# A four-layer attention and Fourier-mixing kernel: another rule for the steps at which QKV groups are issued

## The chip, the cores and the metric

The kernel runs on one core of one Trainium2 chip. The core has five engines with a queue each, worked off in order: TensorE (PE, matmuls and transposes into the eight PSUM banks), VectorE (DVE), ScalarE (ACT), GpSimd (POOL) and SyncE (SP), which issues nearly all DMAs here. The metric is the device time of one execution in microseconds; the time before is the median of 3 runs.

## What is computed

Four layers on x of 2048 x 640 (float32), attention, Fourier, attention, Fourier, each added to its input after a layer norm:

```python
def _A_ref(x, wqkv, wo):          # H = 32 heads of 20, W = 8, dil = 2
    qkv = (x @ wqkv).reshape(B, S, 3, H, Dh)...
    idx = pos[:, None] - (jnp.arange(W) * dil)[None, :]
    logits = jnp.einsum("bhsd,bhswd->bhsw", q, kg) * scale   # kg = k at idx
    logits = jnp.where(mask, logits, -1e9)
    o = jnp.einsum("bhsw,bhswd->bhsd", softmax(logits), vg)
    return o @ wo

def _B_ref(x, re_s, im_s, re_h, im_h):
    a, b = x @ re_h.T, x @ im_h.T
    return re_s @ a - im_s @ b

x = x + _A_ref(_layernorm(x), wqkv, wo)
x = x + _B_ref(_layernorm(x), ...)
x = x + _A_ref(_layernorm(x), wqkv, wo)
x = x + _B_ref(_layernorm(x), ...)
```

Every matmul is made of three passes on operands that are split into a high part and a residue.

## The kernel before

**Tiling.** The sequence is cut into NC = 4 chunks of NJ = 4 tiles of 128 tokens. The QKV weights are cut into NQ = 4 quarters (8 heads each). A *QKV group* is one chunk c, quarter q and tile j: `qkv_mm` (L346) runs 15 matmuls (L356) of 128x480 into PSUM bank m0 or m1 by the parity of the group's number, `qkv_evac` (L359) copies the bank to a staging tile `stg` (two buffers) on ScalarE (L363), and after each second tile `qkv_store` (L365) writes K, V (`kvb`) and Q (`qb`) to DRAM. There are 64 groups in an attention layer.

**Attention units.** A unit u (0 to 31) is one chunk and four heads. `q_load` (L384) and `w_load` (L401) read Q and the eight shifted K or V rows back from DRAM; `q_copy` (L398) puts Q into PSUM bank pq on ScalarE; `qk_mul` (L422) multiplies on VectorE (L425) and adds halves on POOL (L427); `qk_red` (L433), the softmax pieces `soft` (L443 to L459) and `soft_exp` (L441, on ScalarE) follow; `av_mul` (L463) multiplies by V on VectorE and `av_tree` (L478 to L480) sums on POOL.

**Other TensorE work of a layer.** A tile of x is loaded (`x_load`, tag `xa`, two buffers), normalized on ScalarE (`x_norm`, L185), transposed (`tp`: L321 on TensorE, high part L325 on ScalarE, subtraction of it in PSUM L329 on TensorE, residue L344 on ScalarE). The first chunk's tiles are ready ahead of the steps, the twelve of chunks 1 to 3 are transposed at steps `tx[(c, j)]`. The output product `wo_mm` (L503) runs in two halves per tile, two and three steps after the steps in `OUTP`, and `wo_add` (L153) adds its result on VectorE.

**The plan.** Both attention layers are one long list of steps, -7 to 66. `at(step, phase, fn, ...)` enters a piece; at the end, steps are walked in order, and in each step the phases in the order of `PHASES` (L815). This fixes the order on all five engines, SyncE's queue included. Unit u takes steps 2u and 2u + 1 for `qk_mul`, the next ones for softmax and V. `q_copy` of unit u stands in step 2u - 1, in phase `qc`, after the phases `evac`, `hi`, `exp`, `evacA`, `actL`, `evacO`, `actl`, all of which are ScalarE's. A group of an odd step is evacuated in phase `evac` of the next step; a group of an even step in `evacA` of its own step, or, if the group before it has the same step, in `evacO` of the next.

**The steps of groups.** `order` lists the 64 groups; `gs` gets a step for each. The first 16 come from `LEAD0` (layer 0) or `LEAD2` (layer 2). The rest is filled in by the loop over `st`: two groups in an even step, one in an odd step or in a step listed in `THIN`, as soon as the tile's transposes are in an earlier step. Transposes may be placed in even steps, one tile per step, once all groups on that tile's buffer (the same j of the chunk before) are in earlier steps.

```python
            cap = 0 if st < 6 else 2 if st % 2 == 0 and st not in THIN[ly] else 1
            for _ in range(max(0, cap - gs[:16].count(st))):
                if len(gs) < NGRP and len(gs) <= 16 + st and tx.get(order[len(gs)][::2], st) < st:
                    gs.append(st)
```

The loads of unit u stand in steps 2u - 2 (`q_load` in phase `dma`, `w_load` of K in `dmaw`) and 2u + 1 (`w_load` of V); a store of a group from step 6 on stands in phase `dmas`, which comes after `dma` and `dmaw` of the same step.

Of the kernel before, what the change touches and what calls it, by code (L numbers as in the profile page):

```python
# [27 lines left out]
NC = 4  # L28
NJ = 4
NQ = 4  # L30
# [8 lines left out]

THIN = ((20, 24, 26, 28, 32, 36, 40, 44), (12, 16, 20, 24, 28, 32, 36, 44, 48))  # L40
OUTP = (((20, 24, 28, 32), (36, 40, 44, 46)), ((20, 24, 28, 32), (36, 40, 44, 46)))
LNS = ((40, 52), (40, 52))


LEAD2 = (-7, -6, -5, -4, -2, 0, 0, 1, 1, 2, 3, 4, 4, 6, 6, 7)
ZTHIRDS = (
# [27 lines left out]
def tile_layers(ctx: ExitStack, tc: tile.TileContext, x, wqkv, wo, cs, wre, wim, out):  # L74
# [158 lines left out]
    NGRP = NC * NQ * NJ  # L233
    ENGINES = {e.engine for e in (nc.tensor, nc.vector, nc.scalar, nc.gpsimd, nc.sync)}

    def layer_a(li, stats, handoff, prev):
        xin, xout = xs[li], xs[li + 1]
        first = li == 0
        ly = li // 2
# [431 lines left out]
        for k in range(KD):  # L671
# [6 lines left out]
        order = [(0, q, j) for q in range(NQ) for j in range(NJ)]  # L678
        order += [
            (c, 2 * qh + i, 2 * jh + j)  # L680
            for c in range(1, NC)
            for qh in range(2)
            for jh in range(2)
            for i in range(2)
            for j in range(2)
        ]
        gs = list(LEAD0 if first else LEAD2)
        tx = {(0, j): -8 for j in range(NJ)}
        st = 4
        while len(gs) < NGRP:  # L690
            if st % 2 == 0 and len(tx) < NC * NJ:
                c, j = divmod(len(tx), NJ)
                used = [i for i, x in enumerate(order) if x[0] == c - 1 and x[2] == j]
                if used[-1] < len(gs) and gs[used[-1]] < st:
                    tx[(c, j)] = st
            cap = 0 if st < 6 else 2 if st % 2 == 0 and st not in THIN[ly] else 1
            for _ in range(max(0, cap - gs[:16].count(st))):
                if len(gs) < NGRP and len(gs) <= 16 + st and tx.get(order[len(gs)][::2], st) < st:
                    gs.append(st)
            st += 1  # L700
        for g, cqj in enumerate(order):
# [27 lines left out]
        for c in range(1, NC):  # L729
            for j in range(NJ):  # L730
                b = tx[(c, j)]
                at(b - 4, "dma", x_load, c, j)
                if first:
                    at(b - 3, "actl", x_stats, c, j)
                    at(b - 2, "fin", x_fin, c, j)
                at(b - 1, "actl", x_norm, c, j)
                tp(b, "x", c, j, 0, 4, "xt", 0, f"s{j}")
                tp(b, "x", c, j, 4, 5, "t1", 256)
# [602 lines left out]
```

## Time and profile before

| | |
|---|---|
| median of 3 runs | 1803.96 us (1803.42 to 1805.32) |
| the profiled execution, its own time | 1805.26 us |
| its span, first to last instruction | 1803.4 us |
| granted TensorE clock, mean | 0.994 |
| layer 0's attention, T(0) to T(63) | 34.0 to 371.9 us |
| layer 2's attention, T(0) to T(63) | 936.8 to 1263.4 us |
| TensorE busy in the Fourier part, 395 to 900 us | 497.4 of 505 |
| DMA, mean rate | 236 GB/s |

T(s) is the start of step s's L425. A row of busy time by stretch reads: the stretch and its length, then for each engine the busy time and the count of instructions, then the granted clock, the mean busy share of the 16 DMA engines and GB/s. A row of the chain of waits reads: start, duration, and what ran or was waited for. A row of the timeline reads: start, duration, engine, line, operation, out<-in, shape, count, and in brackets the idle time ahead of it with what ended it. Matmuls are pipelined, so a group's time on TensorE is the distance between starts (3.25 us for 15), not the sum of their durations.

### The profile page before, as it was taken

The page shows a single profiled execution, that of the slowest core. Times are in us where ns is not written, and L with a number is a line of the kernel's source. Part 1 is how long each engine was busy: PE and PEld are TensorE (multiplying, and loading weights), DVE is VectorE, ACT ScalarE, POOL GpSimd, SP SyncE. Part 2 cuts the span into 40 slices and gives each one's busy share as a digit, 9 for nine tenths or more (in the row PEclk, how much of TensorE's full clock was granted, in tenths as well). Part 3 has the DMA queues.
Part 4 walks back from the last instruction along what each step waited for, and adds up shares of the span by engine and source line. Part 5 has one row for each costly group of instructions (what it writes and reads, how often), then busy time and mean ns, then how long its engine had stood idle before and what let it go on. Part 6 is the DMA issues. An engine that isn't in the chain of part 4 may idle for free.

```text
span 1803.4 us, 26465 instructions
## 1 busy us (share of the span) xinstructions
PE 1743.7 (97%) x8798; PEld 1505.7 (83%) x8798; DVE 1382.3 (77%) x2129; ACT 816.8 (45%) x1702; POOL 633.5 (35%) x591
## 2 busy tenths in 40 slices
PE   9999997989999999999999999999899999999999
PEld 6878896877888888888888889878787888888888
DVE  5999899887767767767739987889777676676673
ACT  5654544444445445445523434444534443443441
POOL 3899898950000000000018987899300000000000
PEclk9999998999999999999999999999999999999999
DMA  6896667847777787777647766687687766866861
GB/s 238 280 312 209 211 202 245 273 166 280 261 253 254 247 269 253 240 269 256 224 134 232 258 191 194 204 307 260 205 300 264 251 222 228 266 231 221 261 208 52
DMA packets 271849, 425.15 MB, mean 236 GB/s; under 512 B 22592, under 2 KB 150592, under 8 KB 271456
## 3 DMA queue, kind: packets, MB, share of 16 engines
q1 hardware_dynamic: 268512, 421.49, 70.5%
q10 hardware_dynamic: 3200, 1.97, 0.4%
q8 instruction: 70, 1.15, 0.3%
q14 instruction: 67, 0.55, 0.1%
HBM read 338.23 MB, written 85.14 MB: 235 GB/s over the span
## 4 chain that ended last, share of the span: by engine, by line
PE 64%; DVE 13%; DMA 9%; POOL 7%; issue 3%; ACT 3%; SPq 0%; DVEq 0%; ACTq 0%; POOLq 0%
PE m L356 15%; PE aux L1018 12%; PE t L1107 10%; PE m L1107 10%; PE pq L1107 5%; PE xt L1107 5%; PE aux L503 4%; DMA win<-cs_in 3%; DVE pr L425 2%; POOL pr L478 2%; DVE pr L463 2%; DMA xc<-stg 2%; POOL pr L427 2%; POOL r L876 1%; POOL pr L479 1%
## 5 line engine op out<-in xcount | busy, mean ns | idle before, releaser
L356 PE MATMUL m<-r,s 128*128 128x480 f32 x1920 | 438.3, 383 | 7.5 <-ACT stg L363 2.9
L356 PEld LDWEIGHTS m<-r,s 128*128 128x128 f32 x1920 | 355.9, 188 | 63.4 <-ACT stg L363 4.6
L1100 ACT CAST r<-win 128x512 fp32r<-128x512 f32 x248 | 151.6, 620 | 170.4 <-DVE win L1136 79.9
L168 POOL TENSOR_TENSOR stats<-stats,mhalf 128x1 f32<-128x1 f32 (+1 forms) x40 | 28.8, 719 | 564.5 <-ACT stats L164 564.5
L1018 PE MATMUL aux<-r2a,zo 128*128 128x320 f32 x768 | 226.4, 309 | 0.0
L478 POOL TENSOR_TENSOR pr<-pr 128x640 f32<-128x640 f32 x126 | 205.6, 1632 | 40.1 <-DVE pr L463 39.2
L1018 PE MATMUL aux<-pr,zo 128*128 128x320 f32 x704 | 208.2, 308 | 0.0
L425 DVE TENSOR_TENSOR pr<-pq,win 128x1280 f32<-128x1280 f32 x128 | 189.8, 1483 | 23.4 <-ACT pq L398 23.3
L1101 DVE TENSOR_TENSOR r<-win,r 128x512 fp32r<-128x512 f32 x248 | 167.3, 687 | 45.6 <-ACT r L1100 43.9
L463 DVE TENSOR_TENSOR pr<-pq,win 128x1280 f32<-128x1280 f32 x128 | 190.8, 1491 | 4.3
L427 POOL TENSOR_TENSOR pr<-pr 128x640 f32<-128x640 f32 x128 | 183.5, 1434 | 19.1 <-DVE pr L425 16.1
L1107 PE MATMUL m<-r,r 128*128 128x512 f32 x606 | 156.5, 392 | 1.0 <-DVE r L1101 0.9
L1018 PEld LDWEIGHTS aux<-r2a,zo 128*128 128x128 f32 x768 | 144.1, 188 | 2.0
L940 PE MATMUL m<-s,r 128*128 128x512 f32 x384 | 120.0, 400 | 16.6 <-DMA s<-c0b 5.3
L1107 PEld LDWEIGHTS m<-r,r 128*128 128x128 f32 x606 | 113.5, 188 | 26.9 <-DVE r L1101 1.2
L1018 PEld LDWEIGHTS aux<-pr,zo 128*128 128x128 f32 x704 | 132.2, 188 | 2.1
L1107 PE MATMUL t<-r,r 128*128 128x512 f32 x483 | 130.7, 393 | 2.1 <-issue 2.1
L940 PE MATMUL t<-s,r 128*128 128x512 f32 x384 | 118.1, 395 | 2.3 <-DVE ot L1000 1.5
L479 POOL TENSOR_TENSOR pr<-pr 128x320 f32<-128x320 f32 x126 | 113.7, 903 | 9.9
L363 ACT COPY stg<-m 128x480 f32<-128x480 f32 x128 | 71.1, 556 | 100.7 <-PE m L356 89.9
L433 DVE TENSOR_REDUCE lg<-pr 128x64 f32<-128x640 f32 x128 | 103.9, 812 | 13.8 <-POOL pr L427 13.6
L1107 PEld LDWEIGHTS t<-r,r 128*128 128x128 f32 x483 | 90.5, 188 | 23.6 <-issue 1.5
(274 smaller groups left out, 3231.2 us busy)
## 6 DMA issues: line engine op xcount, KB each, us to landing
win<-cs_in SPq DMA_DIRECT2D x354, 256.0 KB, 4.1
r<-xc SPq DMA_DIRECT2D x240, 256.0 KB, 4.2
win<-kvb SPq DMA_DIRECT2D x96, 440.0 KB, 4.7
xa<-cs_in SPq DMA_DIRECT2D x122, 256.0 KB, 3.9
win<-kvb SPq DMA_DIRECT2D x64, 360.0 KB, 5.1
xc<-stg SPq DMA_DIRECT2D x40, 512.0 KB, 4.6
kvb<-stg SPq DMA_DIRECT2D x60, 320.0 KB, 3.2
xr<-xs SPq DMA_DIRECT2D x40, 320.0 KB, 3.9
```

Source lines behind the costliest of these rows:

```text
L356: nc.tensor.matmul(mt[g][:, : 3 * F], st[:, a, k], wq[q][:, b, k], start=n == 0, stop=n == 14)
L425: nc.vector.tensor_tensor(pr, q, wview(u, jp, 0, [[1, FE]]), op=ALU.mult)
L427: nc.gpsimd.tensor_tensor(pv[:, :, 0:10], pv[:, :, 0:10], pv[:, :, 10:20], op=ALU.add)
L433: nc.vector.tensor_reduce(lgs[u][:, 2 * jp : 2 * jp + 2].rearrange("p j w h -> p (j w h)"), prq.pop((u, jp))[:, :, 0:10], axis=AX.X, op=AL ...
L463: nc.vector.tensor_tensor(pr.rearrange("p j w (h d) -> p j w h d", d=DH), lgs[u][:, 2 * jp : 2 * jp + 2].unsqueeze(4).to_broadcast([P, 2, ...
L478: g.tensor_tensor(pr[:, :, 0:4], pr[:, :, 0:4], pr[:, :, 4:8], op=ALU.add)
L479: g.tensor_tensor(pr[:, :, 0:2], pr[:, :, 0:2], pr[:, :, 2:4], op=ALU.add)
L940: self.last = nc.tensor.matmul(self.z[t][k], self.xn[c][:, a, j, k * P : (k + 1) * P], self.ct[s][:, b], start=s == 0 and i == 0, stop=s = ...
L1018: self.last = nc.tensor.matmul(self.ym[e][:, :320], zt[(k, a, ri)][:, j2 * P : (j2 + 1) * P], w[:, e * 320 : (e + 1) * 320], start=(k, a, ...
L1100: nc.scalar.copy(hi, raw)
L1101: nc.vector.tensor_tensor(lo, raw, hi.bitcast(F32), op=ALU.subtract)
L1107: nc.tensor.matmul(bank, w(a, kb), hl[b], start=start and (a, b) == (0, 0), stop=stop and (a, b) == (1, 0),)
```

## The change

It replaces `THIN` by a running sum of TensorE's work. `work` is all that stands in steps 6 to `QKV_END` = 46 (3.25 for a group, 0.83 for a tile's transposes, 0.8 and twice 2.2 for an output tile); `rate` is that by the number of steps; a group is entered into a step as long as the sum stays under the straight line `rate * (st - 5)` plus `AHEAD` = 2.4, at most two in any step, odd or even. `LEAD2` is shifted in three places. In layer 2 a tile's transposes may stand in step 5, 7, 8, 9, 10 and any later step. The order of groups in chunk 1 follows `QJ1`; in chunks 2 and 3 the pair of tiles is the outer loop and the quarter the inner. A tile's load is entered no earlier than the step in which the tile two before it in the chunk is transposed. `PHASES` and all functions that issue instructions are the same.

```diff
-THIN = ((20, 24, 26, 28, 32, 36, 40, 44), (12, 16, 20, 24, 28, 32, 36, 44, 48))
+QJ1 = ((0, 0), (1, 0), (0, 1), (2, 0), (1, 1), (3, 0), (2, 1), (3, 1))
+QKV_END = 46
+AHEAD = 2.4
...
-LEAD2 = (-7, -6, -5, -4, -2, 0, 0, 1, 1, 2, 3, 4, 4, 6, 6, 7)
+LEAD2 = (-7, -6, -5, -4, -2, -1, 0, 0, 1, 2, 3, 4, 4, 5, 6, 7)
...
         order = [(0, q, j) for q in range(NQ) for j in range(NJ)]
-        order += [
-            (c, 2 * qh + i, 2 * jh + j)
-            for c in range(1, NC)
-            for qh in range(2)
-            for jh in range(2)
-            for i in range(2)
-            for j in range(2)
-        ]
+        order += [(1, q, 2 * jh + j) for q, jh in QJ1 for j in range(2)]
+        order += [(c, q, 2 * jh + j) for c in range(2, NC) for jh in range(2) for q in range(NQ) for j in range(2)]
         gs = list(LEAD0 if first else LEAD2)
         tx = {(0, j): -8 for j in range(NJ)}
-        st = 4
-        while len(gs) < NGRP:
-            if st % 2 == 0 and len(tx) < NC * NJ:
+        other = {}
+        for c in range(2):
+            for a in OUTP[ly][c]:
+                for t, w in ((a, 0.8), (a + 2, 2.2), (a + 3, 2.2)):
+                    other[t] = other.get(t, 0) + w
+        work = sum(w for t, w in other.items() if 6 <= t <= QKV_END)
+        work += 3.25 * sum(g >= 6 for g in gs + [NGRP] * (NGRP - len(gs))) + 0.83 * (NC - 1) * NJ
+        rate = work / (QKV_END - 5)
+        done = 0
+        for st in range(4, 60):
+            if (st % 2 == 0 if first or st > 10 else st > 4 and st != 6) and len(tx) < NC * NJ:
                 c, j = divmod(len(tx), NJ)
                 used = [i for i, x in enumerate(order) if x[0] == c - 1 and x[2] == j]
                 if used[-1] < len(gs) and gs[used[-1]] < st:
                     tx[(c, j)] = st
-            cap = 0 if st < 6 else 2 if st % 2 == 0 and st not in THIN[ly] else 1
-            for _ in range(max(0, cap - gs[:16].count(st))):
-                if len(gs) < NGRP and len(gs) <= 16 + st and tx.get(order[len(gs)][::2], st) < st:
-                    gs.append(st)
-            st += 1
+                    done += 0.83
+            n = gs[:16].count(st)
+            if st >= 6:
+                done += other.get(st, 0) + 3.25 * n
+            while st >= 6 and n < 2 and len(gs) < NGRP and tx.get(order[len(gs)][::2], st) < st:
+                if done + 3.25 > rate * (st - 5) + AHEAD:
+                    break
+                gs.append(st)
+                done += 3.25
+                n += 1
+        assert len(gs) == NGRP
...
-                at(b - 4, "dma", x_load, c, j)
+                at(max(b - 4, tx.get((c, j - 2), 0)), "dma", x_load, c, j)
```

## The prediction

> **What bounds the kernel now.** I read the page first, then the busy time by stretch, then the chain of waits in both attention layers, then the order of single instructions where the chain leaves TensorE. "T(s)" below is the start of the first multiplication (L425, `qk_mul`) of step s; a step belongs to one half of one attention unit.
>
> ```profile
> span 1803.4 us, 26465 instructions
> PE 1743.7 (97%) x8798; PEld 1505.7 (83%) x8798; DVE 1382.3 (77%) x2129; ACT 816.8 (45%) x1702; POOL 633.5 (35%) x591
> PE 64%; DVE 13%; DMA 9%; POOL 7%; issue 3%; ACT 3%; SPq 0%; DVEq 0%; ACTq 0%; POOLq 0%
> ```
>
> TensorE holds most of the chain, but not all of it, so stretches have to be looked at by themselves. The next view gives, for each stretch, its length, then busy time of PE, PE's loads, DVE, ACT and POOL, the granted clock and DMA.
>
> ```profile
> 65.02:147.08 82.06, 76.97 (x371) 64.84 (x370) 78.45 (x103) 46.42 (x112) 75.91 (x71) 1.00 0.89 291
> 147.08:228.99 81.91, 81.87 (x440) 73.37 (x439) 73.51 (x108) 42.84 (x117) 73.03 (x70) 1.00 0.65 203
> 147.08:175.07 27.99, 27.99 (x157) 25.58 (x155) 27.27 (x41) 10.90 (x31) 26.21 (x25) 1.00 0.65 203
> 970.76:979.98 9.22, 9.22 (x50) 8.00 (x48) 8.96 (x13) 4.23 (x10) 8.81 (x9) 1.00 0.72 207
> 961.64:1035.17 73.53, 71.09 (x344) 61.50 (x343) 70.90 (x95) 29.44 (x69) 68.77 (x64) 0.98 0.78 253
> 1035.17:1169.31 134.14, 134.14 (x714) 120.57 (x713) 113.20 (x165) 56.72 (x144) 110.77 (x102) 1.00 0.61 195
> 993.17:996.58 3.41, 3.27 (x9) 2.75 (x10) 2.89 (x6) 1.22 (x5) 3.25 (x4) 0.50 0.85 330
> ```
>
> Rows 1 and 2 are steps 6 to 21 and 22 to 37 of layer 0: first VectorE is full (78.45 of 82.06) and TensorE has gaps, then TensorE is full and VectorE has gaps (73.51 of 81.91). Rows 5 and 6 are steps 6 to 21 and 22 to 45 of layer 2, with a much larger contrast (113.20 of 134.14). A pair of steps takes 9.2 us where VectorE sets it (row 4), 9.33 with output additions (row 3: three pairs). So there is something to even out. The chain shows where it turns:
>
> ```profile
> 126.74 2.10 POOL pr L478
> 145.27 3.25 PE m L356 x15
> 222.07 3.28 PE m L356 x15
> 228.99 1.49 DVE pr L425
> ```
>
> In layer 0 it is on VectorE and POOL until step 21 and on TensorE from 145 to 225 us. In layer 2:
>
> ```profile
> 909.90 3.11 PE m L356 x13
> 933.84 13.01 PE m L356 x60
> 983.94 8.17 DMA qb<-stg
> 992.21 0.56 ACT stg L363
> 994.21 20.72 PE m L356 x90
> 1014.93 0.44 PE xt L321 x4
> 1019.00 6.58 PE m L356 x30
> 1158.74 2.19 PE aux L503 x15
> 1161.49 3.26 PE m L356 x15
> 1168.86 0.43 ACT pq L398
> 1169.31 1.49 DVE pr L425
> ```
>
> From 994 to 1164.7 us it is TensorE without a break. A QKV group (15 matmuls, L356) is 3.25 us, half an output product 2.19. What ends it is the evacuation of the one group of step 44, then ScalarE's queue, then `q_copy` (L398) of step 45, then T(46) = 1169.31.
>
> **The change part by part.** The instructions are the same in kind and number; only steps move. I worked the step lists out from the rule itself. Groups finished by the end of a step, before and after:
>
>     step            5   9  12  13  16  21  28  30  36  44  45  47
>     layer 0 before 16  21  24  25  30  36  43  46  53  61  62  64
>     layer 0 after  16  21  25  27  31  38  45  46  53  62  64  64
>     layer 2 before 13  18  21  22  26  33  41  44  51  61  62  64
>     layer 2 after  14  19  24  26  30  37  44  46  53  62  64  64
>
> *Layer 0* is unchanged through step 10. The gaps that can be filled stand in TensorE's own list:
>
> ```profile
> 86.11 2.40 PE L356 MATMUL m<-r,s 128*128 128x480 f32 x10
> 89.86 4.58 PE L356 MATMUL m<-r,s 128*128 128x480 f32 x20 [1.36 <-ACT s L344]
> 96.65 3.54 PE L356 MATMUL m<-r,s 128*128 128x480 f32 x15 [2.20 <-ACT stg L363]
> 100.91 13.36 PE L356 MATMUL m<-r,s 128*128 128x480 f32 x60 [0.72 <-ACT stg L363]
> ```
>
> The first gap waits for a residue that the change doesn't move, and the 2.20 gap (bank m1 until step 12's evacuation) stays too: the second group that step 11 now has ends by about 94.2, in the place of the one that ran there. What goes are the 0.72 and the later pauses up to 145 us (0.5), and the order in steps 12 to 15 leaves no new ones: at 3.25 us a group and 0.83 us a transposed tile I get 37 groups at 145.7, with one tile more transposed; the old kernel had 36 at 144.2 and would have the same work done at 148.5. TensorE is 2.5 us ahead. Against it, step 14 gets two groups; the second is evacuated in step 15 ahead of `q_copy` (L398), at 117.0 rather than 110.7, and T(16) goes from 117.05 to about 120.7. VectorE is then 3.3 behind at step 22 and does steps 22 to 37 at 9.33 a pair plus the same 0.1 of slack: 147.08 + 3.3 + 8 x 9.45 = 226.0; by TensorE T(38) = 228.99 - 2.5 = 226.5. So layer 0 gains 2.5. Bounds: 5.5 gained if T(16) doesn't move (the least that VectorE needs is 147.08 + 75.6 = 222.7, and a little for jitter); 1 lost if both sides lag in turn.
>
> *Layer 2* has another start. Transposes of chunk 1 come in steps 5, 7, 8, 9 and not 6, 8, 10, 12, and step 6 issues groups 14 and 16 (032 and 100, chunk, weight quarter, tile), with 15 in step 7. Both of step 6 use bank m0. The ScalarE rows of the same place before:
>
> ```profile
> 961.18 0.43 ACT L398 COPY pq<-qs 128x320 f32<-128x320 f32 x1
> 965.50 0.31 ACT L441 ACTIVATE lg<-lg 128x128 f32<-128x128 f32 x1 [2.72 <-DVE lg L452]
> 965.72 0.54 ACT L363 COPY stg<-m 128x480 f32<-128x480 f32 x1
> 966.16 0.59 ACT L344 CAST s<-xt 128x512 fp32r<-128x512 f32 x1
> 969.48 0.92 ACT L185 ACTIVATE xa<-xa,stats 128x640 f32<-128x640 f32 x1
> ```
>
> and TensorE's:
>
> ```profile
> 961.33 0.66 PE L321 MATMUL xt<-ident,xa 128*128 128x128 f32 x4 [1.51 <-ACT xa L185]
> 993.31 0.80 PE L329 MATMUL xt<-s,nident 128*128 128x512 f32 x1 [2.44 <-ACT s L325]
> ```
>
> Until 959.9 both kernels give TensorE the same groups in the same order. Then I walk the two queues in the new order:
> - Step 5: tile (1,0) at once (the 1.51 gap goes), group 13 until 963.7, then the subtraction (L329); the residue (L344, 0.75 with its small part) now stands ahead of step 5's `q_copy`, so T(6) is 965.25 and not 961.64.
> - Step 6: group 14 ends at 967.25. Group 16 needs the same bank, and its evacuation stands behind the exponential, 3.86 after T(6): free at 969.9, a stall of 2.65. It ends at 973.2; tile (1,1)'s normalization (L185, 0.92) stands behind its evacuation: a stall of 1.4.
> - Step 7: group 15 until 978.4; residue, then normalization of (1,2), with nothing left on TensorE: 1.65; and `q_copy` behind them makes T(8) 980.8 (before 970.76), which holds bank m1 another 0.45.
> - Step 8: group 17 until 984.55; evacuation, residue, normalization of (1,3): 2.3.
> - Steps 9 to 12: 18 to 22 without a gap, the last (120) done at 1004.15; T(12) 1001.5.
>
> The stalls sum to 8.45. Before lost 1.51 and 2.44 here, and a half clock: the last row of the second fence shows 3.41 us at 0.50, 1.7 us of work. Both orders reach 30 groups and the first tile of chunk 2: before at 1025.59 (1019.00 + 6.58), after, by the walk, at 1027.45. So 1.9 lost. The old 8.17 wait for the store `qb<-stg` is not in the sum again: it is what lies behind the 2.44.
>
> From there TensorE is the bound in both, and up to the group whose evacuation gates T(46) there are 61 groups before and 62 after: another 3.25 lost, since steps 46 and 47, where the old kernel had its last two groups, are paced by VectorE and POOL and hid them. Layer 2: +5.2. VectorE isn't in the way: T(12) 1001.5, 17 pairs at 9.2 and 0.4 for additions and the late residues come to 1165, under 1169.31 + 5.2. Bounds: -2.5 (no stall at all: 1.5 + 2.4 + 1.7 won, 3.25 lost) and +12 (below).
>
> *The order inside chunks* (chunk 1 by `QJ1`, chunks 2 and 3 with the tile pair outside) moves the distance from a unit's last store to its loads (units 8 to 31) from 0 to 16 steps to 2 to 14; the staging buffers see the same pairs. *Stores ahead of loads*: unit 8 of layer 2 loads in step 14, and its last store was in the same step, behind:
>
> ```profile
> 998.47 0.32 SPq L395 DMA_DIRECT2D qs<-qb  x1
> 1004.24 0.38 SPq L372 DMA_DIRECT2D kvb<-stg  x1
> ```
>
> Now the store is in step 12 and the load waits for it, at the longest 8.17 us as in the chain. SyncE's queue stands then, with step 14's `w_load` behind it; the data is wanted at step 15's copy, three steps or 13 us on, so I take nothing. *The later `x_load`* (not before the tile two earlier is transposed): (1,2) is issued in step 5, waits for its `xa` until 960.4, and holds behind it a store and a `w_load` that went at 957 and 958; they are wanted from T(7), about 969, so nothing again, and 2 us if that cover is gone. SyncE has slack since T(8) itself is late.
>
> Sum: -2.5 + 5.2 = **+2.7**. The profiled execution took 1805.26, of it 1803.4 span and 1.9 around it; that is 1.3 over the median, so I add the difference to the median: 1803.96 + 2.7 = **1806.7**.
>
> **The rivals.**
> *A, the line works in both layers* (1796). Step 6's stalls don't come, since ScalarE gets to the evacuation in time, and layer 0's `q_copy` isn't held: -2.5 and -5.5. For it: the two rows of layer 0 differ by only 5 us in VectorE's busy time and 5 us in TensorE's, which fit into each other. Against it: ScalarE's queue is in order, and its 2.72 idle ahead of the exponential shows that an evacuation behind it waits.
>
> *B, the stalls bring the half clock* (1814, slower). The trace has it: a stall of 2.44 at 990.9 was followed by the 3.41 us at 0.50, one of 2.20 in layer 0 was followed by none (1.00 in its row). Four stalls within 20 us of 1.4 to 2.65 stand around that bound; if each costs 1.7, layer 2 loses 6.8 more: 1806.7 + 6.8 = 1813.5. It decides from stalls of about 2.4 on. The Trainium skill ("TensorE: Matmul & The Clock Gate", Part 1: The HAM clock gate) says that the clock is gated to half after an idle window of about 3.4 us, in windows that run freely and don't start with the stall; the trace agrees with the length (3.41) though not with a need for a full idle window, and by a free window each stall has its own chance, so that one of four, +1.7, is as likely as none.
>
> *C, the order doesn't matter* (1804). Where TensorE is the bound, a sum is a sum: the start's stalls equal the old ones, and the 3.25 is paid back by layer 0. For it: the 134.14 us are all TensorE. Then the change evens the plan, not the time.
>
> **How the numbers follow.** The forecast as worked out has 0.46, with its own range 1802 to 1811; A 0.25, B 0.19, C 0.10. Under 0.2% (3.6 us) no change can be told: faster is below 1800.4, slower above 1807.6. The forecast gives 0.02 faster, 0.22 same, 0.22 slower; A 0.23 and 0.02 same; B all slower; C 0.08 same, 0.01 to each side. Sums: faster 0.26, same 0.32, slower 0.42. The range reaches from A to B: 1796 to 1814.
>
> **What would show it.** Right: in layer 2 TensorE waits before the second group of step 6 for ScalarE's `stg`, and before the transposes of (1,1), (1,2), (1,3) for `xa`, together 8 us between 965 and 990; T(12) near 1001; the time from T(46) of layer 0 to the same place in layer 2 unchanged, T(46) 2.5 earlier in layer 0 and the distance T(0) to T(46) of layer 2 about 5 longer. Wrong: TensorE goes through these steps without gaps, T(12) under 992, or a chain of layer 2 that leaves TensorE between steps 12 and 45; more than one stretch at a clock of 0.5 in layer 2's first 12 steps speaks for B.

## The result and the profile after

The changed kernel took 1815.13 us (median of 4 runs, 1812.05 to 1819.06) against 1803.69 for the kernel before beside it: ratio 1.0067, 95% interval 1.0047 to 1.0088. It is slower by 8 to 16 us, where 2.7 were forecast. The profiled execution is at the upper end (1819.06, span 1817.3). In the new file the first multiplication, `qk_mul`, is L427, the QKV multiplications are L358, their evacuation L365, `x_norm` L187, `q_copy` L400.

The page of the changed kernel: the span, the busy times, and the chain by engine.

```profile
span 1817.3 us, 26476 instructions
PE 1749.7 (96%) x8798; PEld 1509.5 (83%) x8798; DVE 1384.5 (76%) x2129; ACT 818.4 (45%) x1702; POOL 632.6 (35%) x591
PE 63%; DVE 14%; DMA 9%; POOL 7%; issue 3%; ACT 3%; SPq 0%; DVEq 0%; ACTq 0%; POOLq 0%
```

Each engine has as many instructions as before. TensorE's busy time is 6 us longer (1743.7 before); about 5 of it is clock, not work (an estimate from the mean granted clock, 0.991 against 0.994 before). The rest is time between instructions.

*Layer 0.* Both kernels agree within 0.03 through T(12). ScalarE's own list in the changed kernel (start, duration, line, operation; in brackets the idle time before it and what ended it):

```profile
100.35 0.54 ACT L365 COPY stg<-m 128x480 f32<-128x480 f32 x1
...
105.13 0.56 ACT L365 COPY stg<-m 128x480 f32<-128x480 f32 x1 [3.60 <-DMA qb<-stg]
...
109.28 0.42 ACT L400 COPY pq<-qs 128x320 f32<-128x320 f32 x1
...
117.50 0.56 ACT L365 COPY stg<-m 128x480 f32<-128x480 f32 x1 [1.86 <-DMA qb<-stg]
...
121.65 0.42 ACT L400 COPY pq<-qs 128x320 f32<-128x320 f32 x1
```

Twice an evacuation waits for a staging buffer whose store is still on its way, and `q_copy`, on which the next step depends, stands behind it. The view of the staging tile, 90 to 150 us, sums these waits (us, times). It knows the landing of only two of the 16 stores; their time from issue to landing is 7.0 and 5.3 (min, median, max):

```profile
  DMA qb<-stg: 5.5, 2
DMA to landing us min/median/max: 5.3/6.2/7.0
```

The same view of the kernel before names no wait for a store.

Counted from T(0), T(14) is 3.63 later than before and T(16) 5.03. VectorE carries that lag until step 33, where the old plan has a long step of its own (T(32) to T(34) 14.23 before, 9.32 now); T(46) of layer 0 is 0.46 later, not 2.5 earlier.

*Layer 2.* TensorE's list in steps 6 to 9:

```profile
972.90 5.09 PE L358 MATMUL m<-r,s 128*128 128x480 f32 x15 [2.45 <-ACT stg L365]
...
979.50 0.66 PE L323 MATMUL xt<-ident,xa 128*128 128x128 f32 x4 [1.51 <-ACT xa L187]
...
985.44 0.66 PE L323 MATMUL xt<-ident,xa 128*128 128x128 f32 x4 [1.60 <-ACT xa L187]
...
993.47 0.71 PE L323 MATMUL xt<-ident,xa 128*128 128x128 f32 x4 [1.83 <-ACT xa L187]
```

These are the four stalls that the prediction walked, with the same releasers. But the group at 972.90 takes 5.09, where 3.5 is usual. The busy time by stretch (length, then PE, PE's loads, DVE, ACT, POOL, the granted clock, DMA) says why:

```profile
966.00:1005.00 39.00, 31.55 (x129) 25.91 (x129) 22.38 (x30) 12.88 (x30) 20.71 (x20) 0.87 0.54 167
973.50:976.90 3.40, 3.40 (x10) 2.85 (x9) 3.27 (x6) 0.00 (x0) 2.88 (x4) 0.51 0.00 0
987.14:990.55 3.41, 3.41 (x11) 2.77 (x10) 3.34 (x6) 0.31 (x1) 2.50 (x2) 0.50 0.93 255
993.95:997.36 3.41, 3.41 (x11) 2.88 (x10) 0.98 (x2) 0.76 (x2) 2.92 (x3) 0.50 0.66 200
```

Three stretches of half clock, each behind one of the stalls. The starts of all multiplications L427 from T(0) on, and from T(12) on (count, durations in ns, first and last start):

```profile
L427 DVE TENSOR_TENSOR pr<-pq,win x47: 1475/1484/1492, 940.0 to 1183.6; 128x1280 f32<-128x1280 f32 x47
L427 DVE TENSOR_TENSOR pr<-pq,win x35: 1475/1484/1492, 1009.6 to 1183.6; 128x1280 f32<-128x1280 f32 x35
```

and the same rows of the kernel before:

```profile
L425 DVE TENSOR_TENSOR pr<-pq,win x47: 1479/1483/1493, 936.8 to 1169.3; 128x1280 f32<-128x1280 f32 x47
L425 DVE TENSOR_TENSOR pr<-pq,win x35: 1479/1483/1493, 989.1 to 1169.3; 128x1280 f32<-128x1280 f32 x35
```

From T(0) to T(46) it is 243.6 against 232.5: 11.1 lost, where 5.2 were forecast. To T(12) 17.2 are lost, and 6.1 come back behind it. T(0) itself is 3.2 later in this execution, with a half clock at 912 ahead of the layer; in the two profiles of the kernel before it lies at 936.8 and 939.2.

### The profile page after: what moved, and what is told of

The parts are those of the page before. It is cut to its first block, busy times and chain, and to the rows that moved or that the text cites. A ratio compares the mean times of both kernels' runs of the same rounds, so it can differ in the third digit from the quotient of the medians.

```text
span 1817.3 us, 26476 instructions
## 1 busy us (share of the span) xinstructions
PE 1749.7 (96%) x8798; PEld 1509.5 (83%) x8798; DVE 1384.5 (76%) x2129; ACT 818.4 (45%) x1702; POOL 632.6 (35%) x591
## 4 chain that ended last, share of the span: by engine, by line
PE 63%; DVE 14%; DMA 9%; POOL 7%; issue 3%; ACT 3%; SPq 0%; DVEq 0%; ACTq 0%; POOLq 0%
PE m L358 16%; PE aux L1028 12%; PE t L1117 9%; PE m L1117 9%; PE pq L1117 5%; PE xt L1117 5%; PE aux L505 3%; DMA win<-cs_in 3%; DVE pr L427 2%; POOL pr L480 2%; DMA xc<-stg 2%; DVE pr L465 2%; POOL pr L429 2%; POOL pr L481 1%; POOL r L886 1%
## 5 line engine op out<-in xcount | busy, mean ns | idle before, releaser
L358 PE MATMUL m<-r,s 128*128 128x480 f32 x1920 | 441.2, 385 | 9.7 <-ACT stg L365 5.1
L358 PEld LDWEIGHTS m<-r,s 128*128 128x128 f32 x1920 | 360.5, 190 | 67.1 <-ACT stg L365 6.6
L427 DVE TENSOR_TENSOR pr<-pq,win 128x1280 f32<-128x1280 f32 x128 | 189.8, 1484 | 40.0 <-ACT pq L400 38.8
L365 ACT COPY stg<-m 128x480 f32<-128x480 f32 x128 | 71.0, 557 | 123.0 <-PE m L358 97.1
```

The lines of the kernel that those rows point to most:

```text
L358: nc.tensor.matmul(mt[g][:, : 3 * F], st[:, a, k], wq[q][:, b, k], start=n == 0, stop=n == 14)
L427: nc.vector.tensor_tensor(pr, q, wview(u, jp, 0, [[1, FE]]), op=ALU.mult)
```

## The experiments

All times of layer 2 below are from its own T(0); "windows" are stretches of half clock between T(0) and T(46). Ratios have their 95% intervals; each batch had its own runs of the kernel before (medians 1803.7 to 1806.5).

    kernel              T(12)  T(38)  T(46)  windows   ratio
    before               52.3  188.2  232.5     1
    changed              69.6  201.5  243.6     3      1.0067 (1.0047 to 1.0088)
    after_again          64.9  196.8  239.0     0      1.0056 (1.0037 to 1.0074)
    l2_even_start        52.3  197.2  239.3     1      1.0041 (1.0026 to 1.0056)
    l2_norm_early        61.3  193.3  235.4     0      1.0045 (1.0027 to 1.0063)
    l2_warm              64.9  196.9  239.0     0      1.0061 (1.0042 to 1.0081)
    l2_tail              69.6  201.5  243.7     3      1.0081 (1.0060 to 1.0102)
    l2_o3                66.4  198.4  240.2     1      1.0066 (1.0054 to 1.0079)
    l2_o3_tail           66.4  198.4  239.1     1      1.0063 (1.0048 to 1.0078)
    l2_o3_late           67.9  199.9  240.2     2      1.0051 (1.0037 to 1.0064)
    l2_norm_tail         62.9  194.8  237.0     1      1.0032 (1.0019 to 1.0045)
    l2_end48             63.3  193.4  238.1     1      1.0027 (1.0013 to 1.0040)
    l2_end48_norm        57.4  187.6  232.3     0      1.0001 (0.9988 to 1.0015)
    l2_end48_norm_o3     57.3  187.4  227.7     0      0.9977 (0.9967 to 0.9987)
    best_both            57.3  187.4  227.7     0      0.9981 (0.9972 to 0.9990)
    before_norm          52.3  187.5  231.8     0      1.0008 (0.9997 to 1.0020)

Layer 2 as before, in the other profiles: T(46) is 231.7 in `l0_rule_only` without a window, 232.2 in `l0_spread` and 232.8 in `before_again` with one each. A version of the rule with its line drawn to step 50 (`l2_end50_norm_o3`) has no time, since its plan deadlocks.

**Layer 0: the rule alone, and with fewer groups in a row.** `l0_rule_only` has the new rule and order in layer 0, layer 2 as before. `l0_spread` adds one condition to it:

```diff
-                    if done + 3.25 > rate * (st - 5) + AHEAD:
+                    if done + 3.25 > rate * (st - 5) + AHEAD or gs.count(st - 1) + n > 2:
```

> The new rule, order and load steps in layer 0 alone; layer 2 is planned as before. Theory (layer 2's first 12 steps lose it all; layer 0 gives back at steps 13 to 16 what it wins at 33 and 37): +0.5 us against before, that is 1804.2, within 1 us. Rival (layer 0's longer steps 13 to 16 are a loss of their own, 4 to 6 us, that layer 2 inherits): +3 or more. Rival of the forecast (layer 0 gains): -2.5.

> The new rule in layer 0 alone, with no more than three groups in two neighbouring steps; layer 2 is planned as before. Theory (layer 0 loses at steps 13 to 16 since three pairs of groups come within two steps, so that ScalarE waits for a staging buffer whose store has not landed, with q_copy behind it): ScalarE's waits for qb<-stg in steps 13 to 16 go, T(16) is at most 1.5 later than before and not 5, and layer 0 ends 2 to 4 earlier than before: 1800 to 1803 where before has 1804. Rival (TensorE's lag itself holds q_copy, by evacuation and normalization ahead of it): T(16) still 3 to 5 late and no gain.

The rule alone: ratio 1.0016 (1.0002 to 1.0029), 3.2 us in the medians, as the rival had it. T(16) is 5.2 later, T(46) of layer 0 2.1 later. With at most three groups in two neighbouring steps: ratio 0.9994 (0.9978 to 1.0010). The staging tile in `l0_spread`, same view and stretch as above, has one wait only, for matmuls:

```profile
  PE m L359: 4.5, 4
```

The wait for `qb<-stg` is gone, though the one store whose landing this view knows took 7.0 too: no third pair of tiles comes within a store's time any more. T(16) is that of before (-0.15). But no gain comes of it: a lag returns in steps 22 to 31 (+5.1) and T(46) is at -0.19. So the staging buffers explain the loss at T(16), and the hoped-for 2 to 4 isn't there without it.

**The start of layer 2.** `l2_even_start` has the old LEAD2 and the transposes in even steps, in layer 2 alone; the rest is the change. `l2_norm_early` puts chunk 1's normalizations ahead of the exponential on ScalarE. `l2_warm` adds 31 multiplications whose result nobody reads in the four stalls. `after_again` is the changed kernel unaltered.

```diff
-                at(b - 1, "actl", x_norm, c, j)
+                at(b - 1, "actl" if first or c > 1 else "norm", x_norm, c, j)
...
-            "peT0 dma evac hi pe peL pe2 fin red0 dma2 qk sA sB av0 sD red1 sE sC exp evacA actL evacO actl sF av1 qc"
+            "peT0 dma evac hi norm pe peL pe2 fin red0 dma2 qk sA sB av0 sD red1 sE sC exp evacA actL evacO actl sF av1 qc"
```

`l2_even_start`:

```diff
-LEAD2 = (-7, -6, -5, -4, -2, -1, 0, 0, 1, 2, 3, 4, 4, 5, 6, 7)
+LEAD2 = (-7, -6, -5, -4, -2, 0, 0, 1, 1, 2, 3, 4, 4, 6, 6, 7)
...
-            if (st % 2 == 0 if first or st > 10 else st > 4 and st != 6) and len(tx) < NC * NJ:
+            if st % 2 == 0 and len(tx) < NC * NJ:
```

`l2_warm`, its fillers:

```diff
+        def fill(n):
+            wb = pt([P, 512], "aux1")
+            for i in range(n):
+                nc.tensor.matmul(wb[:, : 3 * F], nident, wq[0][:, 0, i % KD], start=True, stop=True)
...
+            if not first and g == 16:
+                at(6, "pe", fill, 10)
...
+        for s, n in () if first else ((6, 6), (7, 7), (8, 8)):
+            at(s, "pe3", fill, n)
```

> The new kernel, but layer 2 has the first 16 steps of before (LEAD2) and transposes in even steps only; rule and order stay. As before the change, unit 8's loads of layer 2 go ahead of its last store, so tiles 2 and 3 of that unit hold layer 0's rows. Theory (the odd transposes with the residue and normalization behind each other, and the two groups of step 6 in one bank, cost 8 us of stalls and three half clock stretches): the three stalls before the transposes go, T(12) to T(0) in layer 2 falls from 69.6 to about 52, and the time is +3 to +5 against before (0.5 from layer 0, 3.25 from the group more ahead of T(46)). Rival (what costs is the rule's rate, not its start): still +9 or more.

> The new kernel with one move: in layer 2 the normalization of chunk 1's tiles stands ahead of the exponential, the evacuation and the residue in ScalarE's queue of its step, not behind them. Theory (ScalarE's order makes the stalls ahead of the transposes of (1,1), (1,2), (1,3): 1.5, 1.6 and 1.8): these three go, the 2.45 before the second group of step 6 stays, and with two of three half clock stretches gone the time falls 5 to 8 us below the new kernel's 1815. Rival (the x loads or the SyncE queue are late, not ScalarE): the stalls stay and the time too.

> The new kernel with 30 more matmuls of 128x480, whose result is not used, put into TensorE's queue where it stalls in steps 6 to 8 of layer 2: 10 between the two groups of step 6, 6, 7 and 7 ahead of the transposes of steps 7, 8 and 9. Theory (each stall brings a half clock stretch of 3.41 us, 1.7 us of work, three of them): the stretches at 0.50 between 970 and 1000 go, the stalls stay, filled, and the time falls by 4 to 5. Rival (the half clock takes nothing since ScalarE and VectorE set the pace there): same as the new kernel, or up to 2 us more.

> The new kernel once more, beside the others on one chip. All theories: +9 to +13 against before.

In `l2_warm` TensorE's list has the fillers (L364) where the stalls were:

```profile
970.83 2.36 PE L364 MATMUL aux<-r,nident 128*128 128x480 f32 x10
973.44 3.57 PE L358 MATMUL m<-r,s 128*128 128x480 f32 x15 [0.25 <-ACT stg L370]
976.85 1.47 PE L364 MATMUL aux<-r,nident 128*128 128x480 f32 x6
```

No half clock there, groups of 3.5, T(12) 64.9, and T(46) 4.6 earlier than in the changed kernel's first execution. That looked like the price of the half clock and its cure. But `after_again`, with nothing filled, has the same numbers. Its list, and its clock from T(0) to T(12):

```profile
971.79 3.56 PE L358 MATMUL m<-r,s 128*128 128x480 f32 x15 [2.49 <-ACT stg L365]
...
976.87 0.66 PE L323 MATMUL xt<-ident,xa 128*128 128x128 f32 x4 [1.51 <-ACT xa L187]
...
982.80 0.65 PE L323 MATMUL xt<-ident,xa 128*128 128x128 f32 x4 [1.60 <-ACT xa L187]
...
989.26 0.65 PE L323 MATMUL xt<-ident,xa 128*128 128x128 f32 x4 [1.83 <-ACT xa L187]
```

```profile
938.90:1003.76 64.86, 57.38 (x273) 48.66 (x272) 47.82 (x64) 21.09 (x48) 42.13 (x39) 1.00 0.64 198
```

The same four stalls to 0.04 us, and full clock throughout. Three windows cost 4.65 (243.63 - 238.98), that is 1.55 each. As `l2_warm`'s median did not fall (1816.77 against 1815.91 of `after_again`), filling is no gain that can be told.

What differs between the two executions is where the stalls fall on a raster. In each of the 19 profiles, all stretches of half clock start whole multiples of 3.413 us apart (in the changed kernel 912.01, 973.45, 987.10, 993.93), and the raster's place differs from execution to execution. These are the raster's windows just ahead of the three stretches of the changed kernel, and then, in `after_again`, the two windows between which its raster divides the stall of 2.49:

```profile
970.04:973.45 3.41, 0.96 (x5) 0.50 (x4) 3.38 (x4) 0.76 (x2) 2.67 (x2) 1.00 0.95 304
983.69:987.10 3.41, 1.76 (x11) 1.28 (x10) 1.35 (x1) 3.07 (x7) 0.00 (x0) 1.00 0.11 22
990.52:993.93 3.41, 1.58 (x10) 1.22 (x9) 3.24 (x6) 2.03 (x4) 3.25 (x4) 1.00 1.03 321
```
```profile
967.80:971.21 3.41, 1.50 (x7) 0.95 (x6) 3.34 (x6) 0.23 (x2) 1.78 (x2) 1.00 0.83 243
971.21:974.62 3.41, 2.83 (x13) 2.45 (x14) 3.24 (x6) 0.53 (x2) 3.25 (x4) 1.00 0.25 93
```

TensorE is idle for 2.45, 1.65 and 1.83 of 3.41 us in the first three, for 1.91 and 0.58 in the last two. Counted over all 19 profiles from 20 to 1290 us, every one of the 78 windows at full clock with 1.95 us or more idle was followed by half clock, none of the 4465 with less than 1.35, and 28 of the 117 between. So what decides is how much idle time falls into one window of the raster; in the range between, idle time alone does not settle it.

`l2_norm_early` took three of the four stalls down (what is left of them is 0.86 at most); the 2.49 ahead of the second group of step 6 stays. Its rows, from T(0) and from T(12):

```profile
L427 DVE TENSOR_TENSOR pr<-pq,win x47: 1473/1484/1492, 945.3 to 1180.7; 128x1280 f32<-128x1280 f32 x47
L427 DVE TENSOR_TENSOR pr<-pq,win x35: 1473/1483/1492, 1006.6 to 1180.7; 128x1280 f32<-128x1280 f32 x35
```

T(12) is 3.6 earlier than in `after_again`, T(46) too. From T(12) to T(46) it is 174.1, the same as in the changed kernel with three windows (1183.6 - 1009.6 = 174.0), in `after_again` and in `l2_warm`: what the start loses or wins, stalls and half clocks alike, arrives at T(46) undiminished. The total did not follow: its median, 1814.68, is 1.2 below that of `after_again`, not 5 to 8, and that is within the scatter.

`l2_even_start` has T(12) as before, and still T(46) at 239.3: with 21 instead of 24 groups by then the new rule needs 187 from there, a stall of 2.05 and one window included. The median is 7.3 above before, where 3 to 5 were expected. So the old start under the new rule is no cure.

**The last groups.** The prediction put 3.25 on a 62nd group ahead of T(46). `l2_tail` puts layer 2's last four groups back into steps 44 to 47; `l2_o3` puts chunk 3's groups in the old order; `l2_o3_tail` does both; `l2_o3_late` has the old order and the old steps for the last eight.

```diff
         assert len(gs) == NGRP
+        if not first:
+            gs[60:] = (44, 45, 46, 47)
```
```diff
+        if not first:
+            order[48:] = [(3, 2 * qh + i, 2 * jh + j) for qh in range(2) for jh in range(2) for i in range(2) for j in range(2)]
```
```diff
+            gs[56:] = (41, 42, 42, 43, 44, 45, 46, 47)
```

> The changed kernel in both layers, with one thing put back: layer 2's last four groups in steps 44, 45, 46 and 47 as before, so that 61 and not 62 groups stand ahead of T(46). Theory (the gate of T(46) moved by one group, about 6 us with the output halves beside it): T(46)-T(0) of layer 2 falls from the 239.0 that the changed kernel had in the execution without a half clock to about 233 (232 to 234), 5 more for each execution that has the half clock in its start; the total falls by 4 to 6, to a ratio of about 1.003 to 1.004. Rival (the extra time ahead of T(46) belongs to the start alone, 8.45 of stalls): T(46)-T(0) stays at 237 or more without any half clock and the total does not fall.

> The changed kernel with one thing put back: chunk 3 of layer 2 in the old order, so that the last group of weight quarter 0 is not the 58th, in step 41, but the 54th, in step 37. Theory (two gates, one behind the other: the cast into quarter 0's buffer at T(42), and the 62nd group at T(46)): T(42)-T(0) of layer 2 falls from the 218.5 that the changed kernel has without half clocks in its start to 214 to 216, but T(46)-T(0) stays at about 238 to 239, since the 62nd group still stands ahead of it; total as the changed kernel within 2. Rival (the cast at T(42) alone sets T(46), VectorE paces the rest): T(46)-T(0) falls by as much as T(42), to about 235. Each execution with half clocks in the start has up to 5 more.

> The changed kernel with both put back in layer 2: chunk 3 in the old order and the last four groups in steps 44 to 47. Theory (two gates, so only both together help): T(42)-T(0) of layer 2 214 to 216 and T(46)-T(0) 234 to 236 without half clocks in the start (changed kernel 239.0), total 3 to 5 below the changed kernel, ratio about 1.003 to 1.004. Rival (the loss is TensorE's work in the start, so its place later on doesn't matter): T(46)-T(0) at 238 or more.

> The changed kernel in both layers; in layer 2 chunk 3 in the old order, and its last eight groups (57 to 64) in the old steps 41, 42, 42, 43, 44, 45, 46, 47. Start, line and order are the change's up to step 39. Theory (T(42) is gated by the number of groups ahead of it, 57 to 59 against 55 to 57, and VectorE takes 20.4 from there): T(42)-T(0) falls from 218.3 (l2_o3 less its half clock) to 211 to 214, and T(46)-T(0) to 232 to 235 without half clocks in the start, 1.6 more for each, TensorE being the gate again. Rival (the start's stalls are what is lost): T(46)-T(0) stays at 237 or more without half clocks.

The theory fell each time: T(42) or T(46) did not come down to where it put them. `l2_tail` from T(12) on:

```profile
L427 DVE TENSOR_TENSOR pr<-pq,win x35: 1475/1485/1492, 1011.3 to 1185.3; 128x1280 f32<-128x1280 f32 x35
```

174.0 again: the 62nd group behind T(46) gains nothing. The chain of waits in `after_again` (start, duration, engine, tile, line; the shortest pieces are left out) shows what holds T(46) besides it:

```profile
1151.59 3.28 PE m L358 x15
1155.04 0.54 issue
1155.58 0.30 ACT stats L160 x2
1155.90 0.93 ACT junk L162 x2
1156.97 0.43 ACT pq L400
1157.42 1.49 DVE pr L427
...
1174.35 1.49 DVE pr L465
1175.84 0.77 DVE r L886
1176.61 0.54 issue
1177.15 0.81 DVE lg L435
1177.95 1.40 DVE pr L427
```

The chain is TensorE's without a break from 994.9 to 1154.9. It leaves TensorE not at step 44, as before, but ahead of T(42) = 1157.42; from there it is mostly VectorE's. In `l2_tail`, `l2_o3`, `l2_o3_tail` and `l2_o3_late` T(42) to T(46) takes 20.4 as well (23.4 before). Rows from T(38) to T(46), before and then `l2_o3_late`, in which TensorE's late groups were out of the way:

```profile
L425 DVE TENSOR_TENSOR pr<-pq,win x9: 1479/1486/1493, 1125.0 to 1169.3; 128x1280 f32<-128x1280 f32 x9
```
```profile
L427 DVE TENSOR_TENSOR pr<-pq,win x9: 1475/1484/1492, 1140.4 to 1180.6; 128x1280 f32<-128x1280 f32 x9
```

44.3 and 40.2; VectorE is busy for 39.2 of the 40.2. No profile of layer 2 is under 40.2 there; layer 0 before has 40.3. So at most 4.1 can be won back behind T(38), and T(38) is 8.6 late in `after_again` (196.8 against 188.2), with 53 groups issued by step 36 where the old plan has 51. Less its windows (1.55 each), `l2_o3_late` is at 237.1, 1.9 better than `after_again`, still 4.5 behind before and 5.4 behind an old layer 2 without a window (231.7).

The late T(38) comes from these two groups and the start. From T(12) to T(38) TensorE of `after_again` has no gap, while VectorE is busy for 117.9 of 131.9:

```profile
1003.76:1135.70 131.94, 131.94 (x687) 117.39 (x686) 117.90 (x166) 54.99 (x138) 114.66 (x106) 1.00 0.70 221
```

The last evacuation ahead of T(38)'s `q_copy` in ScalarE's queue, in the kernel before and in `after_again`, starts when TensorE has ended the 51st group (1120.51) and the 53rd (1133.32):

```profile
1120.59 0.56 ACT L363 COPY stg<-m 128x480 f32<-128x480 f32 x1 [2.33 <-issue]
```
```profile
1133.40 0.56 ACT L365 COPY stg<-m 128x480 f32<-128x480 f32 x1 [2.34 <-issue]
```

Two groups are 6.5, and the 30th group ends 2.3 later after T(0) (91.1 against 88.8): 8.8 by this estimate, 8.6 measured.

**Versions.** Two further edits to the rule in layer 2, with layer 0 as before: the line drawn to step 48 (`QKV_END = 48`, in `l2_end48`), with the early normalizations (`l2_end48_norm`), and with chunk 3 in the old order (`l2_end48_norm_o3`). `l2_norm_tail` has the line to 46, early normalizations and the last four groups late. `before_norm` is the kernel before with the early normalizations alone; `best_both` is `l2_end48_norm_o3` with the layer 0 of `l0_spread`. The edits beside those already shown:

```diff
-QKV_END = 46
+QKV_END = 48
...
-            order += [(c, q, 2 * jh + j) for c in range(2, NC) for jh in range(2) for q in range(NQ) for j in range(2)]
+            order += [(2, q, 2 * jh + j) for jh in range(2) for q in range(NQ) for j in range(2)]
+            order += [(3, 2 * qh + i, 2 * jh + j) for qh in range(2) for jh in range(2) for i in range(2) for j in range(2)]
```

> Layer 0 as before; layer 2 with the new rule, start and order, but the line ends at step 48 (QKV_END = 48). The rule then puts group 16 behind group 15 in step 7, so step 6 has one group, and 60 groups stand ahead of T(46), not 62. Theory (the groups ahead of T(46) add up, since TensorE is the bound there; the bank stall and the residue stall of (1,2) go): T(46) to T(0) in layer 2 falls from 243.6 to between 232 and 236 (before: 232.5), time 0 to +4 against before. Rival (TensorE's sum up to step 46 does not count, only the start's stalls): 238 or more.

> As l2_end48, with the normalization of chunk 1's tiles in layer 2 ahead of the exponential in ScalarE's queue. Theory: none of the stalls of steps 6 to 9 is left over 1 us, T(46) to T(0) is 225 to 230 (before: 232.5), and the time is 2 to 6 below before. Rival (VectorE or the loads bound it once TensorE has no stalls): 232 or more, no gain.

> Layer 0 as before. Layer 2 by the new rule and order, with chunk 1's normalizations put ahead of the exponential on ScalarE and the last four groups in steps 44 to 47. Theory (the loss of layer 2 is three stalls behind the exponential and one group ahead of T(46), and nothing else): T(46)-T(0) of layer 2 about 229 to 230 (before 232.5), total 2 to 4 below before, ratio 0.998 to 0.999. Rival (the time after T(46) is VectorE's and POOL's and takes back what is won, or a wait comes that the trace doesn't show yet): T(46) earlier by 2 or more but the total within 1 us of before.

> Layer 0 as before. Layer 2 by the new rule to step 48 with the early normalizations, and with chunk 3's groups in the old order, so that the last groups of weight quarter 0 come in steps 37 and 38 and not in step 41, where the rounded layer-norm rows in their buffer waited for them (4.87 on ScalarE). Theory: that wait goes, T(42) no longer jumps, T(46)-T(0) of layer 2 falls below before's 232.5 by 3 to 6 (226 to 229), total 2 to 5 below before. Rival: T(42) keeps its jump of about 3, so the wait was not from the order of chunk 3, and the total stays that of before.

> The kernel before with the old plan and old order everywhere, but with chunk 1's normalizations of layer 2 ahead of the exponential. It tells whether the gain of l2_end48_norm_o3 (ratio 0.9977) is the rule's. If the early normalizations alone make it: T(12)-T(0) of layer 2 2 to 4 less than before, T(46)-T(0) about 228 and a ratio of about 0.998. If the rule's line makes it: T(46)-T(0) within 2 of before's 232.5, ratio 0.999 to 1.000. Estimate: the gap of 1.5 to 1.9 before tile (1,0) can go, the one of 2.7 before the correction of (1,3) waits for another cast and stays, so 1 to 2 us are gained.

> Layer 2 as in l2_end48_norm_o3 (line to step 48, early normalizations of chunk 1, chunk 3 in the old order), and layer 0 by the new rule with at most three groups in two neighbouring steps as in l0_spread. Theory (the two layers add): T(46) of layer 0 as before within 0.5, T(46)-T(0) of layer 2 about 227.7, ratio 0.997 to 0.998, the same as l2_end48_norm_o3 (0.9977). Rival: the layers' order in the layer between makes a difference, ratio 0.999 or more.

Taken in this order, each edit brings its part. `l2_end48` is at 236.5 less its window, just above its 232 to 236. `l2_end48_norm` is at 232.3, its rival's value. From `l2_norm_early` to it, both without windows, T(46) falls by 3.1, with a new wait: ScalarE's rounding of a layer-norm row into the buffer that held weight quarter 0 waits for that quarter's last group, which the new order of chunk 3 puts into step 41.

```profile
1147.05 0.73 ACT L908 CAST r<-xa 128x640 fp32r<-128x640 f32 x1 [4.87 <-PE m L359]
```

In `l2_end48_norm_o3` chunk 3 is in the old order, quarter 0's last group is in step 38, and the wait is gone; its T(0) to T(46) and T(38) to T(46):

```profile
L428 DVE TENSOR_TENSOR pr<-pq,win x47: 1475/1484/1492, 938.7 to 1166.3; 128x1280 f32<-128x1280 f32 x47
L428 DVE TENSOR_TENSOR pr<-pq,win x9: 1475/1483/1490, 1126.1 to 1166.3; 128x1280 f32<-128x1280 f32 x9
```

227.7, 4.8 less than before, and the last four pairs at VectorE's 40.2. It is a clear gain, if a small one: 1801.68 (median of 12) against 1806.47, ratio 0.9977 (0.9967 to 0.9987). Only `best_both`, which has the same layer 2, gains as well. It is not the early normalizations alone: under the old plan (`before_norm`) they give 231.8, as an old layer 2 without a half clock has (231.7 in `l0_rule_only`), and no gain in the median. `l2_norm_tail` missed its 229 to 230 by seven, one window included. `best_both` adds nothing to `l2_end48_norm_o3` (0.9981); layer 0's mended rule is worth nothing that can be told.

**The kernel before once more.**

> The kernel before once more, unchanged, for the half clock: how many stretches of 3.41 us at 0.50 this execution has and where, and how far two executions of the same code differ. If the half clock is drawn anew in each execution, the places differ from those of the first profile (303.7, 993.2, 1198.0, 1252.6) and the span differs by some us; if it follows from the stalls alone, they are the same. The ratio is 1.000 within 0.0015.

Ratio 1.0003 (0.9989 to 1.0016), runs from 1799.93 to 1812.32. Its window in the start of layer 2:

```profile
996.66:1000.07 3.41, 3.41 (x10) 2.83 (x9) 2.87 (x6) 0.56 (x2) 3.06 (x4) 0.50 0.66 262
```

It stands behind the same stall as in the first profile (993.2), with T(0) 2.4 later; the window at 911.3 ahead of the layer is new, the one at 1252.6 is gone. So the places of risk are the kernel's, and which of them are hit is the execution's, by its raster.

## Why the prediction was off

The sign and the order of the parts were right in layer 2, and the sum was too small by 8 to 9. Two terms failed: layer 0's gain of 2.5, and the half clock, which was put at nothing. Layer 2 without half clock came out near its term, but one step of its working is wrong.

*Layer 0, -2.5: failed.* The step is "the staging buffers see the same pairs". They see the same pairs, but closer together: six groups in steps 11 to 13 where the old plan has four, with two buffers and stores that land after up to 7.0. That is the wait of 3.60 and 1.86 on ScalarE, and T(16) came at 122.1 and not 120.7. Steps 22 to 37 then took 77.3, not the 75.6 of the working. TensorE was ahead as computed in kind (the 37th group 1.5 earlier; the working takes 2.5, though its own 148.5 - 145.7 is 2.8), but T(46) came 0.46 later, 2.1 in `l0_rule_only`, and 3.2 where a half clock fell on steps 12 and 13 (`after_again`). The bound named for "both sides lag in turn" (1 lost) was the nearer one; `l0_spread` shows that also without the wait nothing was to be won.

*Layer 2, the start: right.* The four stalls came at their places, behind the instructions named, and T(12) at +12.5 without half clock, +12.4 in the walk. The stalls' sum is paid in full, as `l2_norm_early` shows. The 30th group ended 2.3 later, 1.9 in the walk.

*Layer 2, T(46): near in size at full clock, wrong in its reason, and so near by luck.* +6.5 in `after_again` against +5.2. "From there TensorE is the bound in both" holds up to T(42). The step that failed is the one behind it, 3.25 for a 62nd group ahead of T(46): `l2_tail` moved that group and nothing came back. In its place two groups more ahead of T(38) make it 8.6 late, and VectorE, which takes the last four pairs at its own 40.2 to 42.2 where the old plan had 44.3, can't win all of it back. The check in the prediction that "VectorE isn't in the way" took 17 pairs at 9.2 from T(12) in one sum, as if VectorE could use every moment in which TensorE holds it up; it has to be asked at each step. Two entries of its step table are off by one, and nothing rests on them: 32 and not 33 groups of layer 2 by step 21 before, 47 and not 46 of layer 0 by step 30 after. Its lower bound for layer 2 adds up to -2.35, not -2.5.

*The half clock: rival B, right in mechanism, wrong in its point of decision.* "It decides from stalls of about 2.4 on" doesn't hold: stalls of 1.6 and 1.8 were followed by windows in one execution, and in another no stall was. The price was 1.55 each and not 1.7. The Trainium skill ("TensorE: Matmul & The Clock Gate", Part 1: The HAM clock gate) says that the clock drops after at least one idle window of about 3.4 us, and that these windows run freely. The raster above agrees with windows that run freely. It does not agree with the need for a whole idle window, since 1.95 of 3.41 us were always enough, and the measurement decides. That each stall then has its own chance is the prediction's conclusion, and the six profiles with this start bear it out: 3, 0, 3, 1, 1 and 2 windows. One of four, +1.7, was taken there to be as likely as none, and so the forecast's +2.7 had no half clock in it; the mean here is 10/6 windows, 2.6 us. That rival B's total, 1814, lies near the measured 1815 is luck: it put 6.8 on layer 2's windows and kept layer 0's gain.

In sum, an estimate: without windows layer 0 loses 0.5 (to 0.8 in four of the five profiles without a window at 97 us, 2.1 in the fifth) and layer 2, at T(63), 5.3 (`after_again` against `before`, whose own window is in it). Layer 2's windows add 2.6. Layer 0's window cost 2.7 (3.2 - 0.5) and fell in 5 of the 10 profiles of the new layer 0, so 1.35 on the mean. That is 9.8 of the 11.4 between the medians. The rest is not told apart from the scatter between executions, whose times span 12 us in `before_again`.

*The order inside chunks and the stores ahead of loads* were put at nothing. Unit 8's loads cost nothing that shows: T(12) to T(16), with its first use, takes 18.4 in `after_again` and 18.7 before. The change does more there than the working says: in the old layer 2 its loads of Q and K are issued at 998.47 and 999.36 and the stores of its last two tiles only at 1004.24 and 1004.71, so that unit 8 read for these tiles what layer 0 had left in the same buffers. The new plan stores first. The order had a price that the prediction didn't see, the wait for quarter 0's buffer; in the line to step 46 it is hidden (`l2_o3` without its window is 0.3 better than `after_again`), in the line to 48 it costs 4.6.

## What to carry to other kernels

Evening out one engine's work over steps moves the steps themselves: ask at each step which engine gates it and how fast the other can go from there, since an engine that was made to wait early can't win back more than its own floor allows. A group that is moved takes its evacuation, its staging buffer and its store with it; two more in neighbouring steps need a buffer that is free for a store's whole time. And before a kernel is credited with a few us for avoiding half clock, look at a second execution of the kernel without the cure: the stalls are the same, and the raster they fall on is not.

## What the hardware showed beside this

Stretches of 3.41 us at a clock of 0.50 came behind stalls of 1.6 to 2.5 us in some executions and not in others of the same code. They lie on a raster of 3.41 us whose place differs from execution to execution, and follow a window of it with 1.95 us or more without TensorE work (78 of 78), at a price of 1.55 us each in the new layer 2 and of 0.5 to 1.1 in the old one. In layer 0 the old plan absorbs such a stretch at 97 us (T(46) of layer 0 within 0.1 of before in `l2_end48` and `l2_end48_norm`), the new plan pays 2.7 for it. Two profiles of one kernel differ by 4.65 us at T(46) for this reason alone, so that one profile of each kernel could not have told the changes apart; T(s) counted from the layer's own start, with its windows named, could.
